# Last column chunk in pieces of 256, 128 and 128, and bulk loads split to choose the lane of the last store

## The chip, the cores and the metric

One core of a Trainium2 chip runs the whole program. The metric is the device time of one execution in microseconds (us); lower is better. The time is 1.9 us longer than the span of the trace (214.39 against 212.46 us for the profiled run of the kernel before). The kernel before took 214.23 us at first sight (median of 3 runs, 214.21 to 214.36). The experiments ran in three batches, each on one chip (a on chip 6; b1, b3, b4 and c on chip 1; b2 and d on chip 15), each with fresh runs of the kernel before.

## The reference

The input x has 2048 rows of 512 columns. Each row is layer-normalized to xn, and the output is x + A(xn) + B(xn):

```python
# A: a diagonal state-space model, 512 complex states, step over the 2048 rows
h = Lam_bar * h + Bu[t]                       # Bu = xn @ B_bar.T
y = 2.0 * (hseq @ Cmat.T).real + xn * Dskip
# B: a gated feed-forward layer with F = 1792
out = (silu(xn @ w1) * (xn @ w3)) @ w2
```

Inputs and output are bfloat16.

## The kernel before

The rows are worked on in four blocks of 512. For each block TensorE computes gate and up (`gu_ps`), the state input (`bu_ps`), and then the output (`y_ps`): per chunk of 128 rows, 14 matmuls of the feed-forward layer and 8 of the state are summed in one PSUM tile. VectorE adds the residual to the tile and a DMA stores it. The last chunk of the last block has nothing behind it that could hide its add and its store, so the kernel before already splits it into two column halves:

```python
        def finish(cl, dsl=slice(0, D), eng=nc.sync):
            o = outp.tile([P, D], BF16, name="o")
            nc.vector.tensor_tensor(out=o[:, dsl], in0=tiles[cl][:, dsl], in1=xn_blk[b][:, cl, dsl], op=ALU.add)
            eng.dma_start(out=ov[:, b * CPB + cl, dsl], in_=o[:, dsl])

        if b == NBLK - 1:
            # ... (chunks 0 to 2, whole)
            for i in range(2):
                dsl = slice(i * D // 2, (i + 1) * D // 2)
                from_gate(CPB - 1, dsl)      # 14 matmuls, own weights for each
                from_state(CPB - 1, dsl)     # 8 matmuls
                finish(CPB - 1, dsl, nc.sync if i == 0 else nc.scalar)
            return
```

The loads that matter here are issued on the SyncE queue; the DMA transposes of block 1 (`xnT<-xn`, four of them) follow them on the same queue:

```python
    def bulk_loads():
        # ... (w1, w3, x block 1, transposed B and C)
        nc.sync.dma_start(out=w2_sb, in_=B_w2.rearrange("(t p) d -> p t d", p=P))
        nc.sync.dma_start(out=dskip_row, in_=A_Dskip.partition_broadcast(P))

    def late_loads():        # issued after the transposes of block 1
        load_x(2)
        load_x(3)
```

Each DMA that SyncE or ScalarE issues signals its landing on one of eight semaphores. In the built instructions they are taken in turn, so the n-th DMA has lane n modulo 8. At the end of the program SyncE waits for all eight in a fixed order: lane 1, 2 (with 0), 3, 4, 5, 6, 7. The order is given by the framework; which lane the last store has depends only on how many DMAs were issued before it.

Of the kernel before, what the change touches and what calls it, by code (L numbers as in the profile page):

```python
# [16 lines left out]
P = 128  # L17
# [34 lines left out]
def kernel(  # L52
# [17 lines left out]
    nc = tc.nc  # L70
    _, S, D = A_x.shape
    F = B_w1.shape[1]
    PS = A_Lambda_re.shape[0]
    CPB = 4
# [5 lines left out]
    NFT = F // P  # L80
    LN_EPS = 1e-5
    FIRST = 3
    MID = 8
    NWARM = 9
    assert S == NBLK * TBLK and D == NDT * P and F == NFT * P and PS == NPT * P

    xv = A_x[0].rearrange("(c p) d -> p c d", p=P)
# [19 lines left out]
    w2_sb = const.tile([P, NFT, D], BF16, name="w2_sb")  # L107
# [17 lines left out]
    x_blk = [xpool.tile([P, CPB, D], BF16, name="x_blk") for _ in range(NBLK)]  # L125
# [3 lines left out]
    def load_w(f0, f1, eng1=nc.sync, eng3=nc.sync):  # L129
        eng1.dma_start(out=w1_sb[:, :, f0:f1], in_=w1v[:, :, f0:f1])  # L130
        eng3.dma_start(out=w3_sb[:, :, f0:f1], in_=w3v[:, :, f0:f1])

    def load_x(b):
        nc.sync.dma_start(out=x_blk[b], in_=xv[:, b * CPB:(b + 1) * CPB, :])

    for c in range(CPB):
        eng = nc.sync if c % 2 == 0 else nc.scalar
# [6 lines left out]
    def bulk_loads():  # L144
        nc.vector.tensor_copy(out=w1_sb[:, 0, FIRST * P:FIRST * P + 1], in_=mv_all[:, 1, 0:1])  # L145
        load_w(FIRST * P, MID * P)
        load_x(1)
        nc.sync.dma_start_transpose(out=bt_re, in_=A_B_re)
        nc.sync.dma_start_transpose(out=bt_im, in_=A_B_im)
        load_w(MID * P, 11 * P)  # L150
        load_w(11 * P, F)
        nc.sync.dma_start_transpose(out=ct_re, in_=A_C_re)
        nc.sync.dma_start_transpose(out=ct_im, in_=A_C_im)
        nc.sync.dma_start(out=w2_sb, in_=B_w2.rearrange("(t p) d -> p t d", p=P))
        nc.sync.dma_start(out=dskip_row, in_=A_Dskip.partition_broadcast(P))

    def late_loads():
        load_x(2)
        load_x(3)


    warm = const.tile([P, TBLK], BF16, name="warm")
# [3 lines left out]
    def keep_busy(n, cols):  # L166
        for _ in range(n):
            nc.tensor.matmul(out=wps[:, 0:cols], lhsT=warm[:, 0:P], rhs=warm[:, 0:cols], start=True, stop=True)

    keep_busy(NWARM, TBLK)  # L170
    nc.scalar.preload_act_table_set("natural_log_exp_and_others")
# [263 lines left out]
    def glu(b):  # L435
# [25 lines left out]
        if b == 0:  # L461
# [11 lines left out]
            ln_stats(0, 1)  # L473
            ln_first_rstd(1)
            bulk_loads()
            ln_apply(0, 0)
            ln_first_transpose(0)()
# [61 lines left out]
    def y(b):  # L539
        tiles = {}  # L540

        def from_gate(cl, dsl=slice(0, D)):
            if cl not in tiles or dsl.start:
                tiles[cl] = ps_y.tile([P, D], FP32, name="y_ps")
            for f in range(NFT):
                nc.tensor.matmul(out=tiles[cl][:, dsl], lhsT=hg_blk[b][:, f, cl * P:(cl + 1) * P],  # L546
                                 rhs=w2_sb[:, f, dsl], start=(f == 0), stop=False)

        def from_state(cl, dsl=slice(0, D)):
            for ri, ct in ((0, ct_re), (1, ct_im)):  # L550
                for pt in range(NPT):
                    nc.tensor.matmul(out=tiles[cl][:, dsl], lhsT=h_blk[b][:, pt, ri, cl * P:(cl + 1) * P],  # L552
                                     rhs=ct[:, pt, dsl], start=False, stop=(ri == 1 and pt == NPT - 1))
# [7 lines that stand above are left out]
            bg.flush(("ssm", b))  # L561
            bg.flush(("res", b))
            for cl in range(CPB - 1):
                from_gate(cl)
                from_state(cl)
                finish(cl)
            for i in range(2):
                dsl = slice(i * D // 2, (i + 1) * D // 2)
                from_gate(CPB - 1, dsl)
                from_state(CPB - 1, dsl)  # L570
                finish(CPB - 1, dsl, nc.sync if i == 0 else nc.scalar)
            return

        for cl in range(0, CPB, 2):
            from_gate(cl)
            bg.fill(2.8)
            from_gate(cl + 1)
            bg.fill(2.4)
            if cl == 0:
                bg.flush(("ssm", b))  # L580
                bg.flush(("res", b))
            from_state(cl)
            finish(cl)
            bg.fill(1.0)
            from_state(cl + 1)
            finish(cl + 1)
            bg.fill(1.0)
# [12 lines left out]
    bg.flush(("ln", 1))  # L600
    gate()
    late_loads()
    finish_c = [weight_c(pt) for pt in range(NPT)]
    res_tasks(0)
# [6 lines left out]
    bu(1)  # L611
    ln_scalar_engine(2)
    y(0)
    ssm_tasks(2)
    res_tasks(2)
    bu(2)
    gate = glu(2)
    gate()
    ln_scalar_engine(3)
    y(1)  # L620
    ssm_tasks(3)
    res_tasks(3)
    bu(3)
    gate = glu(3)
    gate()
    y(2)
    y(3)

# [29 lines left out]
```

## Time and profile before

| | value | where it stands |
|---|---|---|
| span | 212.46 us | page |
| TensorE busy | 207.2 us, 98% | page, part 1 |
| share of TensorE in the chain that ended last | 94% | page, part 4 |
| granted clock | 1.0 | page and runs |
| last matmul starts, end of span | 208.93, 212.46 us | records of the trace |

These lines of the page of the kernel before give the span, each engine's busy time and count, the chain that ended last by engine, and the stores (bytes of one, us from issue to landing); the last line, for the last store alone, is from the full list of DMA issues:

```profile
span 212.5 us, 2774 instructions
PE 207.2 (98%) x1056; PEld 99.0 (47%) x1056; DVE 155.7 (73%) x186; ACT 116.3 (55%) x219; POOL 24.7 (12%) x50
...
PE 94%; ACT 1%; DMA 1%; DVE 1%; issue 0%
...
out_dram<-o SPq DMA_DIRECT2D x15, 128.0 KB, 1.7
...
out_dram<-o ACTq DMA_DIRECT2D x1, 64.0 KB, 1.6
```

TensorE works almost all the time. A change can therefore gain only by shortening its stream, or what stands before its first or after its last matmul.

The timeline of the end of the kernel before (start, duration, engine, line, operation, output and input, count, and in brackets the idle time before it and what ended it):

```profile
206.63 1.69 PE L546 MATMUL y_ps<-w_sb,hgT 128*128 128x256 bf16 x14
206.83 0.42 DVE L557 TENSOR_TENSOR o<-y_ps,xn 128x256 bf16<-128x256 f32 x1 [1.71 <-PE y_ps L552]
207.29 0.33 SPq L558 DMA_DIRECT2D out_dram<-o  x1
...
208.60 0.60 PE L552 MATMUL y_ps<-ct_im,h 128*128 128x256 bf16 x4
209.24 0.42 DVE L557 TENSOR_TENSOR o<-y_ps,xn 128x256 bf16<-128x256 f32 x1 [1.98 <-PE y_ps L552]
209.69 0.37 ACTq L558 DMA_DIRECT2D out_dram<-o  x1
```

After the last matmul come an add of 0.42 us, the issue of a store, and then nothing that is counted as work, up to 212.46. What happens there can be read from the semaphore records of the same trace. "Lane" is the semaphore's place in the rotation; each line is the moment at which SyncE passed a wait:

```
209.693  last store issued (ACT queue), signals lane 3
211.269  the 16th and last of its landing signals arrives
211.286  SyncE passes lane 3
211.355  SyncE passes lane 4     (signalled long ago)
211.422  SyncE passes lane 5     (signalled long ago)
211.486  SyncE passes lane 6     (signalled long ago)
211.548  SyncE passes lane 7     (signalled long ago)
211.613  SyncE passes one more wait
211.688  SyncE gives its signal to the closing barrier
212.455  end of the span
```

The store takes 1.58 us from issue to landing. And the wait that it satisfies is followed by four others that were satisfied long before, and still take 0.062 to 0.069 us each, as SyncE reads them one after another.

### The profile page before, as it was taken

To read this page: it belongs to the slowest core of one execution; us is meant where nothing else is said; L and a number is where in the kernel's file an instruction comes from. 1 tells how busy PE (TensorE), PEld (TensorE's weight loads), DVE (VectorE), ACT (ScalarE), POOL (GpSimd) and SP (SyncE) were. 2 spreads that over 40 slices of the span, in tenths; PEclk is the share of its full clock that TensorE was granted. 3 is DMA by queue.
4 is the path that set the end of the run, shared out by engine and by line. 5 is a ranking of instruction groups with operands and counts; after the bars stand their busy time and mean duration, and the time that the engine had idled before them with its cause. 6 is when DMAs were issued, how large, how long until landed. Compare 5 with 4: busy or idle time off the path is not lost.

```text
span 212.5 us, 2774 instructions
## 1 busy us (share of the span) xinstructions
PE 207.2 (98%) x1056; PEld 99.0 (47%) x1056; DVE 155.7 (73%) x186; ACT 116.3 (55%) x219; POOL 24.7 (12%) x50
## 2 busy tenths in 40 slices
PE   7899999999999999999999999999999999999993
PEld 2874444444444444444444444444444444444462
DVE  3599799999938969899999897828999981121111
ACT  3699897799866764066666786036667620000000
POOL 7170289300000020000000012000000000000000
PEclk9999999999999999999999999999999999999999
DMA  6999999900000003400000001510000000100100
GB/s 167 323 227 213 287 286 213 244 2 0 3 0 0 0 0 77 98 25 0 0 0 5 0 0 25 123 52 0 2 0 0 3 0 3 46 25 29 48 25 26
DMA packets 26797, 13.68 MB, mean 64 GB/s; under 512 B 16544, under 2 KB 26784, under 8 KB 26784
## 3 DMA queue, kind: packets, MB, share of 16 engines
q1 hardware_dynamic: 25200, 12.78, 25.6%
q10 hardware_dynamic: 1488, 0.72, 1.2%
q8 instruction: 8, 0.13, 0.2%
q14 instruction: 5, 0.04, 0.1%
q0 software_dynamic: 96, 0.00, 0.0%
HBM read 7.74 MB, written 2.10 MB: 46 GB/s over the span
## 4 chain that ended last, share of the span: by engine, by line
PE 94%; ACT 1%; DMA 1%; DVE 1%; issue 0%
PE gu_ps L442 45%; PE y_ps L546 23%; PE y_ps L552 13%; PE bu_ps L370 12%; DMA x_blk<-in_A_x_dram 1%; PE bu_ps L442 1%; PE y_ps L209 1%; DVE stats L189 1%; ACT xnT L210 1%; ACT u L372 1%; ACT tabe L337 0%; DVE o L557 0%; DVE mv_all L190 0%; DVE xn L194 0%; DVE w_sb L145 0%
## 5 line engine op out<-in xcount | busy, mean ns | idle before, releaser
L442 PE MATMUL gu_ps<-xnT,w_sb 128*128 128x512 bf16 (+1 forms) x488 | 96.7, 358 | 0.2 <-ACT xnT L210 0.2
L442 PEld LDWEIGHTS <-w_sb 128*128 128x128 bf16 x520 | 46.9, 98 | 50.3 <-issue 0.4
L546 PE MATMUL y_ps<-w_sb,hgT 128*128 128x512 bf16 (+1 forms) x238 | 50.2, 366 | 0.0
L557 DVE TENSOR_TENSOR o<-y_ps,xn 128x512 bf16<-128x512 f32 (+1 forms) x17 | 11.2, 657 | 36.0 <-PE y_ps L552 36.0
L546 PEld LDWEIGHTS <-hgT 128*128 128x128 bf16 x238 | 23.3, 98 | 25.3
L372 ACT ACTIVATE u<-bu_ps 128x512 bf16<-128x512 f32 x32 | 19.1, 597 | 24.2 <-PE bu_ps L370 24.2
L406 DVE TENSOR_TENSOR_SCAN u<-rho,h,u 128x512 bf16<-128x512 f32 x24 | 29.5, 1270 | 0.2
L552 PEld LDWEIGHTS <-h 128*128 128x128 bf16 x136 | 13.3, 98 | 14.3
L552 PE MATMUL y_ps<-ct_re,h 128*128 128x512 bf16 (+1 forms) x68 | 16.6, 366 | 0.0
L552 PE MATMUL y_ps<-ct_im,h 128*128 128x512 bf16 (+1 forms) x68 | 16.6, 366 | 0.0
L370 PE MATMUL bu_ps<-xnT,bt_re 128*128 128x512 bf16 x64 | 16.4, 379 | 0.1
L370 PE MATMUL bu_ps<-xnT,bt_im 128*128 128x512 bf16 x64 | 16.4, 379 | 0.0
L393 DVE TENSOR_TENSOR p<-u,tabe 128x2048 bf16<-128x2048 bf16 x8 | 9.8, 1221 | 3.5 <-ACT u L372 3.4
L242 POOL TENSOR_SCALAR acc<-acc 128x4 f32<-128x4 f32 x2 | 1.0, 502 | 80.1 <-ACT xn L241 80.1
L411 DVE TENSOR_TENSOR p<-u,tabe 128x2048 bf16<-128x2048 bf16 x8 | 9.8, 1224 | 0.2
L418 DVE TENSOR_TENSOR h<-h,p 128x2048 bf16<-128x2048 bf16 x8 | 9.8, 1223 | 0.2
L396 DVE TENSOR_TENSOR u<-u,tabe 128x2048 bf16<-128x2048 bf16 x8 | 9.8, 1222 | 0.2
L400 DVE TENSOR_TENSOR u<-u,p 128x2048 bf16<-128x2048 bf16 x8 | 9.8, 1225 | 0.1
L370 PEld LDWEIGHTS <-bt_re 128*128 128x128 bf16 x64 | 6.3, 98 | 7.8 <-issue 0.3
L370 PEld LDWEIGHTS <-bt_im 128*128 128x128 bf16 x64 | 6.3, 98 | 7.5
L414 DVE TENSOR_TENSOR h<-u,tabe 128x2048 bf16<-128x2048 bf16 x8 | 9.8, 1219 | 0.0
L406 DVE TENSOR_TENSOR_SCAN u<-rho,u 128x512 bf16<-128x512 f32 x8 | 9.3, 1210 | 0.1
(172 smaller groups left out, 197.9 us busy)
## 6 DMA issues: line engine op xcount, KB each, us to landing
out_dram<-o SPq DMA_DIRECT2D x15, 128.0 KB, 1.7
w_sb<-in_B_w_dram SPq DMA_DIRECT2D x1, 1792.0 KB, 9.9
x_blk<-in_A_x_dram SPq DMA_DIRECT2D x3, 512.0 KB, 5.5
w_sb<-in_B_w_dram SPq DMA_DIRECT2D x4, 384.0 KB, 4.9
w_sb<-in_B_w_dram SPq DMA_DIRECT2D x2, 640.0 KB, 6.3
x_blk<-in_A_x_dram ACTq DMA_DIRECT2D x2, 128.0 KB, 3.1
x_blk<-in_A_x_dram SPq DMA_DIRECT2D x2, 128.0 KB, 2.7
w_sb<-in_B_w_dram SPq DMA_DIRECT2D x1, 256.0 KB, 5.8
```

The costliest lines, as they stand in the source:

```text
L370: nc.tensor.matmul(out=ps, lhsT=bt[:, dt, pt * P:(pt + 1) * P], rhs=xnT_blk[b][:, dt, :], start=(dt == 0), stop=(dt == NDT - 1))
L372: nc.scalar.activation(out=u[:, j, ri, :], in_=ps, func=ACT.Copy)
L393: nc.vector.tensor_tensor(out=st["p"], in0=st["g"], in1=tabe[:, psl, 1:3, :], op=ALU.mult)
L396: nc.vector.tensor_tensor(out=st["g"], in0=st["g"], in1=tabe[:, psl, 0:1, :].to_broadcast(FULL), op=ALU.mult)
L400: nc.vector.tensor_tensor(out=st["g"], in0=st["g"], in1=st["p"][:, :, ::-1, :], op=ALU.subtract)
L406: nc.vector.tensor_tensor_scan(out=v, data0=rho[:, pt:pt + 1].to_broadcast([P, TBLK]), data1=v, initial=init, op0=ALU.mult, op1=ALU.add)
L411: nc.vector.tensor_tensor(out=st["p"], in0=st["g"], in1=tabe[:, psl, 1:3, :], op=ALU.mult)
L414: nc.vector.tensor_tensor(out=h_blk[b][:, psl, :, :], in0=st["g"], in1=tabe[:, psl, 0:1, :].to_broadcast(FULL), op=ALU.mult)
L442: nc.tensor.matmul(out=ps[:, tsl], lhsT=w[:, dt, f * P:(f + 1) * P], rhs=xnT[:, dt, tsl], start=(dt == 0), stop=(dt == NDT - 1))
L546: nc.tensor.matmul(out=tiles[cl][:, dsl], lhsT=hg_blk[b][:, f, cl * P:(cl + 1) * P], rhs=w2_sb[:, f, dsl], start=(f == 0), stop=False)
L552: nc.tensor.matmul(out=tiles[cl][:, dsl], lhsT=h_blk[b][:, pt, ri, cl * P:(cl + 1) * P], rhs=ct[:, pt, dsl], start=False, stop=(ri == 1 an ...
L557: nc.vector.tensor_tensor(out=o[:, dsl], in0=tiles[cl][:, dsl], in1=xn_blk[b][:, cl, dsl], op=ALU.add)
```

## The change

The intent: a narrower last piece has a shorter add and a smaller store at the end, where nothing hides them. And with four more DMAs at or before the last store (w2 in two, x blocks 2 and 3 in two each, one more store), the last store moves four lanes on, from lane 3 to lane 7, the lane that is asked last. The other lanes can then be read while the store is still in flight.

```diff
+    LAST_COLS = ((0, D // 2), (D // 2, 3 * D // 4), (3 * D // 4, D))
...
-    def load_x(b):
-        nc.sync.dma_start(out=x_blk[b], in_=xv[:, b * CPB:(b + 1) * CPB, :])
+    def load_x(b, parts=1):
+        n = CPB // parts
+        for i in range(0, CPB, n):
+            nc.sync.dma_start(out=x_blk[b][:, i:i + n, :], in_=xv[:, b * CPB + i:b * CPB + i + n, :])
...
-        nc.sync.dma_start(out=w2_sb, in_=B_w2.rearrange("(t p) d -> p t d", p=P))
+        w2v = B_w2.rearrange("(t p) d -> p t d", p=P)
+        for sl in (slice(0, NFT // 2), slice(NFT // 2, NFT)):
+            nc.sync.dma_start(out=w2_sb[:, sl, :], in_=w2v[:, sl, :])
...
-        load_x(2)
-        load_x(3)
+        load_x(2, 2)
+        load_x(3, 2)
...
-            for i in range(2):
-                dsl = slice(i * D // 2, (i + 1) * D // 2)
+            for lo, hi in LAST_COLS:
+                dsl = slice(lo, hi)
                 from_gate(CPB - 1, dsl)
                 from_state(CPB - 1, dsl)
-                finish(CPB - 1, dsl, nc.sync if i == 0 else nc.scalar)
+                finish(CPB - 1, dsl, nc.scalar if hi == D else nc.sync)
```

## The prediction

> **What bounds the kernel now.** TensorE. The page has PE busy 207.2 of 212.5 us (98%); the chain that ended last is 94% PE; granted clock 1.0. So only what lengthens the PE stream, or stands after its last matmul, moves the time. The end, from the timeline with the trace's DMA landings and semaphore records (us from the span's start):
> - last 128x256 matmul starts 208.93; VectorE's last add starts 209.24, takes 0.42;
> - its store is issued on the ACT queue at 209.69; packets (128 of 512 B, 27 ns each) run 210.56 to 210.92; landed at 211.27, 1.58 us after issue;
> - SyncE's closing waits, about 0.067 us apart: 211.29, .36, .42, .49, .55, a drain at .61, the barrier signal at .69. DMA semaphores rotate over eight lanes, asked in lane order; the last store is on the first of these lanes, so four others, long satisfied, are read after it;
> - barrier and clean-up to 212.46.
> About 3.2 us after the last matmul that PE cannot hide.
>
> **What the change does.**
> 1. Lanes. w2 in two loads, x blocks 2 and 3 in two each, one more store: the last store moves four lanes on. In the built order it uses lane 7 instead of 3, the last one asked, so the other four are read while it is in flight: minus 4 x 0.067 = 0.27 us, all on the critical path.
> 2. Last add 128 wide instead of 256: 0.69 us at 512 columns, 0.42 at 256, so on that line about 0.29: minus 0.13.
> 3. Store rows of 256 B: packets of 256 B took 18 ns elsewhere in this trace against 27, eight per engine: minus 0.07 (estimate); the rest of the 1.58 us stays. The Trainium skill ("DMA: Bandwidth & Descriptors", Specifications) says that below 512 B the DMA does a read-modify-write; no store here is that small yet, so this could eat the 0.07 or more.
> 4. PE: 44 matmuls of 128 columns for 22 of 256. Spacing in this trace: 0.0558 us (opening quarters, weights loaded for each) against 0.1092: plus 0.05. The skill ("TensorE: Matmul & The Clock Gate", Back-to-back issue gap) gives about 81 ns at 128 with weight loads; the trace shows 56, which I use. At 81 the change would lose 1.1 us.
> 5. Loads: same bytes. The split of w2 puts one more issue (about 0.6 us on SyncE) ahead of block 1's four transposes. They land by 39.53 and TensorE begins that block at 39.77: only 0.2 us of slack. The queue is backed up by w2's data there, so I expect little (mean 0.05, at worst 0.5). The x loads have 30 us of slack.
>
> Sum: -0.27 - 0.13 - 0.07 + 0.05 + 0.05 = about -0.4: **213.85 us**, range 213.6 to 214.25. Faster by over 2%: 0.5%; within 2%: 99%; slower by over 2%: 0.5%.
>
> **What would show it.** (1) Landing of the last store to SyncE's barrier signal 0.15 us instead of 0.42, to the end of the span 0.92 instead of 1.19. (2) Last add near 0.29. (3) Issue to landing near 1.5. (4) 128-column matmuls 0.056 apart, no gap between pieces; the third piece waits neither for its output buffer (the first piece's store lands near 208.8, needed 209.3) nor for PSUM. (5) No PE gap near 39.8.
>
> **What would make it wrong.** 128-column matmuls spaced by weight loads; a slow 256 B store; a stall of block 1 behind the split w2; a chip that differs by 0.1 us.

## The result

213.94 us (median of 6 runs, 213.66 to 214.15), against 214.27 us before (6 runs, 214.21 to 214.39). The ratio is 0.9984, 95% interval 0.9971 to 0.9997. Ratios in this document are the mean time of one kernel's fast runs over that of the other's fast runs of the same rounds, so not quite the ratio of the medians quoted. By the line of 2% that the prediction uses, the two kernels count as the same.

The predicted 213.85 us missed by 0.09 us. The effect is small and single runs scatter as much, so that close an agreement is partly luck, and the traces have to say whether the reasons were right.

The lines of the changed kernel's page (and list of DMA issues) that answer to those shown of before:

```profile
span 212.0 us, 2826 instructions
PE 206.5 (97%) x1078; PEld 98.8 (47%) x1078; DVE 155.9 (74%) x187; ACT 116.3 (55%) x219; POOL 24.6 (12%) x50
...
PE 94%; DVE 2%; DMA 1%; ACT 1%; issue 0%
...
out_dram<-o SPq DMA_DIRECT2D x15, 128.0 KB, 1.7
...
out_dram<-o ACTq DMA_DIRECT2D x1, 32.0 KB, 1.5
```

TensorE has 22 matmuls more (1078 against 1056) and is still the chain. The timeline of the end of the changed kernel, in the same columns as before:

```profile
206.63 0.94 PE L551 MATMUL y_ps<-w_sb,hgT 128*128 128x128 bf16 x14
206.83 0.42 DVE L562 TENSOR_TENSOR o<-y_ps,xn 128x256 bf16<-128x256 f32 x1 [1.71 <-PE y_ps L557]
...
208.06 0.29 DVE L562 TENSOR_TENSOR o<-y_ps,xn 128x128 bf16<-128x128 f32 x1 [0.80 <-PE y_ps L557]
...
208.86 0.39 PE L557 MATMUL y_ps<-ct_im,h 128*128 128x128 bf16 x4
209.29 0.29 DVE L562 TENSOR_TENSOR o<-y_ps,xn 128x128 bf16<-128x128 f32 x1 [0.94 <-PE y_ps L557]
209.61 0.37 ACTq L563 DMA_DIRECT2D out_dram<-o  x1
```

The last add is 0.29 us instead of 0.42. The third piece's add waited for TensorE alone, as the bracket says; the landing signals of the first piece's store, whose buffer it reuses, were complete at 208.81. The semaphore records of the same trace, as above:

```
208.758 to 209.009  SyncE passes lanes 1 to 5, while the store is not yet issued
209.612  last store issued (ACT queue), signals lane 7
209.849  SyncE passes lane 6 (the second piece's store)
211.104  the last of the landing signals of lane 7 arrives
211.121  SyncE passes lane 7
211.186  SyncE passes one more wait
211.255  SyncE gives its signal to the closing barrier
212.028  end of the span
```

From the landing to the barrier signal it is now 0.151 us instead of 0.419. The four reads have moved out of the way, as intended.

The upper part of the two traces differs at one place. First the kernel before, the chain that ended last in order of time (start, duration, what):

```profile
27.68 1.89 PE bu_ps L370 x8
29.57 34.53 PE gu_ps L442 x160
64.10 6.91 PE bu_ps L370 x32
```

Then the changed kernel:

```profile
27.57 1.89 PE bu_ps L375 x8
29.45 34.65 PE gu_ps L447 x160
64.10 6.91 PE bu_ps L375 x32
```

The changed kernel came to 29.45 us 0.12 us earlier and lost it again before 64.10. The records of single matmuls show where. They run 0.216 us apart, but between 39.435 and 39.768 us lies one interval of 0.333 us, 0.117 too much. The matmul at 39.768 is the first of block 1. The last transpose of block 1 had landed at 39.677. In the kernel before it landed at 39.525 and was needed at 39.767, so there was no gap. The 0.12 us at the start belongs to the run, not to the kernel, as the 14 traces below show.

### The profile page after: what moved, and what is told of

Read it like the earlier page. It is cut to its first block, busy times and chain, and to the rows that moved or that the text cites. A ratio compares the mean times of both kernels' runs of the same rounds, so it can differ in the third digit from the quotient of the medians.

```text
span 212.0 us, 2826 instructions
## 1 busy us (share of the span) xinstructions
PE 206.5 (97%) x1078; PEld 98.8 (47%) x1078; DVE 155.9 (74%) x187; ACT 116.3 (55%) x219; POOL 24.6 (12%) x50
## 4 chain that ended last, share of the span: by engine, by line
PE 94%; DVE 2%; DMA 1%; ACT 1%; issue 0%
PE gu_ps L447 45%; PE y_ps L551 23%; PE y_ps L557 13%; PE bu_ps L375 12%; DMA x_blk<-in_A_x_dram 1%; DVE stats L194 1%; PE bu_ps L447 1%; ACT u L377 1%; PE y_ps L214 0%; DVE xn L199 0%; ACT tabe L342 0%; ACT xnT L215 0%; DVE mv_all L195 0%; DVE o L562 0%; DVE w_sb L148 0%
## 5 line engine op out<-in xcount | busy, mean ns | idle before, releaser
L551 PE MATMUL y_ps<-w_sb,hgT 128*128 128x512 bf16 (+2 forms) x252 | 50.4, 355 | 0.0
L457 ACT ACTIVATE u<-gu_ps 128x512 bf16<-128x512 f32 x55 | 33.3, 605 | 11.4 <-PE gu_ps L447 10.8
L456 ACT ACTIVATE g<-gu_ps 128x512 bf16<-128x512 f32 x55 | 33.1, 602 | 9.5 <-PE gu_ps L447 9.5
L562 DVE TENSOR_TENSOR o<-y_ps,xn 128x512 bf16<-128x512 f32 (+2 forms) x18 | 11.3, 629 | 35.8 <-PE y_ps L557 35.8
L463 DVE TENSOR_TENSOR hgT<-g,u 128x1024 bf16<-128x1024 bf16 x28 | 19.0, 682 | 5.8 <-ACT u L457 5.8
L557 PE MATMUL y_ps<-ct_im,h 128*128 128x512 bf16 (+2 forms) x72 | 16.8, 355 | 0.0
L557 PE MATMUL y_ps<-ct_re,h 128*128 128x512 bf16 (+2 forms) x72 | 16.8, 355 | 0.0
```

The source lines that it names most:

```text
L456: nc.scalar.activation(out=g16[:, f % 2, :], in_=g_ps, func=ACT.Silu)
L457: nc.scalar.activation(out=u16[:, f % 2, :], in_=u_ps, func=ACT.Copy)
L463: nc.vector.tensor_tensor(out=hgT[:, f - 1:f + 1, :], in0=g16, in1=u16, op=ALU.mult)
L551: nc.tensor.matmul(out=tiles[cl][:, dsl], lhsT=hg_blk[b][:, f, cl * P:(cl + 1) * P], rhs=w2_sb[:, f, dsl], start=(f == 0), stop=False)
L557: nc.tensor.matmul(out=tiles[cl][:, dsl], lhsT=h_blk[b][:, pt, ri, cl * P:(cl + 1) * P], rhs=ct[:, pt, dsl], start=False, stop=(ri == 1 an ...
```

## The experiments

All traces can be compared piece by piece once the start is taken out. The first matmul of the feed-forward part (`gu_ps`) began between 6.90 and 7.33 us in the 14 traces, though nothing of the change stands before it. It is 7.16 and 6.90 for the kernel before and for b2 below, which differs from it only later, and 7.04, 7.18 and 7.26 in three traces of the changed kernel. So the start scatters from run to run, by as much as the effect. From that matmul to the end of the span, the traces repeat within about 0.02 us, also on another chip: 205.293 and 205.284 for the kernel before and b2, 204.863 and 204.878 for the two traces of the changed kernel without a gap.

The traces also say what the start is made of. The first chunk of x landed between 3.24 and 3.52 us. From that landing to the first `gu_ps` matmul it took 3.64 to 3.65 us in the seven traces whose clock records show TensorE's full clock granted by 5.81 us, and longer the later that moment came: 3.67 with 6.00, 3.81 with 6.38, 3.93 with 7.20. (In the trace of before, warm-up matmuls of 512 columns started 0.427 us apart ahead of that moment; later ones of 512 columns start 0.216 us apart.) This is an agreement over 14 traces. No run was made to test it.

The table below has this stretch and its parts, all in us, read from the records of the traces:

| run | pieces; lane of last store | first `gu_ps` to last matmul's start | last matmul's start to add | last add | store, issue to landing | landing to SyncE's barrier signal | first `gu_ps` to end |
|---|---|---|---|---|---|---|---|
| before | 256, 256; 3 | 201.764 | 0.310 | 0.425 | 1.576 | 0.419 | 205.293 |
| changed | 256, 128, 128; 7 | 201.989 (gap 0.117) | 0.256 | 0.292 | 1.492 | 0.151 | 204.985 |
| a1_pieces_only | 256, 128, 128; 4 | 201.877 | 0.257 | 0.292 | 1.497 | 0.328 | 205.055 |
| a2_lanes_only | 256, 256; 7 | 201.769 | 0.309 | 0.425 | 1.571 | 0.145 | 205.019 |
| a3_w2_whole | 256, 128, 128; 7 | 201.877 | 0.256 | 0.291 | 1.491 | 0.140 | 204.855 |
| a4_lane_first | 256, 128, 128; 1 | 201.879 | 0.256 | 0.292 | 1.515 | 0.522 | 205.269 |
| c_after_again | as changed | 201.877 | 0.257 | 0.292 | 1.492 | 0.140 | 204.863 |
| b1_w2_late | 256, 128, 128; 7 | 201.879 | 0.257 | 0.292 | 1.489 | 0.145 | 204.860 |
| b3_best | 384, 128; 7 | 201.824 | 0.257 | 0.292 | 1.435 | 0.140 | 204.744 |
| b4_last64 | 256, 192, 64; 7 | 201.901 | 0.232 | 0.224 | 1.462 | 0.151 | 204.776 |
| d1_best64 | 256, 192, 64; 7 | 201.901 | 0.231 | 0.224 | 1.413 | 0.140 | 204.709 |
| d2_last32 | 256, 224, 32; 7 | 202.116 | 0.213 | 0.192 | 1.437 | 0.145 | 204.903 |
| b2_before_w2_late | 256, 256; 3 | 201.768 | 0.311 | 0.424 | 1.574 | 0.407 | 205.284 |
| d3_after_third | as changed | 201.879 | 0.257 | 0.292 | 1.496 | 0.151 | 204.878 |

What is left in each row is the time from the add's end to the issue of the store (0.03) and from the barrier signal to the end (0.77, the same in all).

The main theory was that of the prediction: the gain is the sum of the lane (0.27), the add (0.13) and the store (0.08), less 0.05 of TensorE. The first rival gives everything to the narrow piece and nothing to the order of the waits; a second gives it to the finer loads. For the gap near 39.8 us, theory S blamed the split of w2.

### a1_pieces_only: the column pieces without the split loads

```diff
-        for sl in (slice(0, NFT // 2), slice(NFT // 2, NFT)):
-            nc.sync.dma_start(out=w2_sb[:, sl, :], in_=w2v[:, sl, :])
+        nc.sync.dma_start(out=w2_sb, in_=B_w2.rearrange("(t p) d -> p t d", p=P))
...
-        load_x(2, 2)
-        load_x(3, 2)
+        load_x(2)
+        load_x(3)
```

> The column pieces 256, 128, 128 alone; all loads as before, so the last store moves one lane on (lane 4), and three lanes stay to be read after it. Main theory (closing waits cost 0.067 us for each lane read after the last store): last add 0.29 us (-0.13), store 1.49 us instead of 1.58 (-0.08), PE +0.05, one lane less -0.07: about -0.23 us against before, near 214.05; landing of the last store to SyncE's barrier signal 0.35 us. Rival (order of the waits is worth nothing, the narrow last piece is all of the gain): -0.33 us, the same time as the changed kernel. No PE gap near 39.8 us, as w2 is one load.

Measured: 214.18 us against 214.42 before in the same rounds, ratio 0.9990 (0.9978 to 1.0002); by the trace 0.24 us less than before from the first `gu_ps` matmul to the end. The add, the store and TensorE are those of the changed kernel, but landing to barrier signal is 0.328, as three lanes are still read afterwards. The pieces alone are not all of the gain; the rival falls. No gap near 39.8 us.

### a2_lanes_only: the lane without the pieces

```diff
-    LAST_COLS = ((0, D // 2), (D // 2, 3 * D // 4), (3 * D // 4, D))
+    LAST_COLS = ((0, D // 2), (D // 2, D))
...
-        load_x(2, 2)
-        load_x(3, 2)
+        load_x(2, 4)
+        load_x(3)
```

> Two pieces of 256 as before, but loads split (w2 in two, x block 2 in four) so that the last store is on lane 7, asked last. Main theory: landing to SyncE's barrier signal 0.15 us instead of 0.42, so -0.27 us in the tail, add 0.42 and store 1.58 unchanged; PE may lose 0.1 us near 39.8 as w2 is split: -0.17 to -0.27 against before. Rival (lane order worth nothing): 0.

Measured: 214.19 us against 214.42, ratio 0.9992 (0.9980 to 1.0004); by the trace 0.27 us less than before. The timeline of its end shows the same work as the kernel before:

```profile
208.54 0.60 PE L557 MATMUL y_ps<-ct_im,h 128*128 128x256 bf16 x4
209.18 0.42 DVE L562 TENSOR_TENSOR o<-y_ps,xn 128x256 bf16<-128x256 f32 x1 [1.98 <-PE y_ps L557]
209.64 0.36 ACTq L563 DMA_DIRECT2D out_dram<-o  x1
```

Add and store cost what they cost before (0.425 and 1.571), and the 0.27 us stands entirely between landing and barrier signal: 0.145 instead of 0.419. The two intervals of the whole times of a1 and a2 reach 1, so it is the traces that separate these effects and not the times. w2 is split here, and there is no gap near 39.8 us.

The parts add up: a1 gained 0.24, of which 0.09 is its own step of one lane (0.419 to 0.328), so the pieces are worth 0.15; with the 0.27 of a2 that is 0.42. The changed kernel without a gap (c_after_again) gained 205.293 - 204.863 = 0.43.

### a4_lane_first: the lane that is asked first

```diff
-        load_x(3, 2)
+        load_x(3, 4)
```

> As the changed kernel, but x block 3 in four loads instead of two: the last store is on lane 1, the one asked FIRST. Wrong on purpose. Main theory: six lanes are read after it instead of none, +0.40 us against the changed kernel, landing to SyncE's barrier signal about 0.55 us instead of 0.15; total near or above before. Rival (finer bulk loads are what helps): the same time as the changed kernel or faster.

Measured: 214.68 us against 214.42, ratio 1.0031 (1.0003 to 1.0059; one of its six runs took 216.58, which pulls the mean up). By the trace it is 205.269 from the first `gu_ps` matmul to the end, 0.02 us under before; what made that run longer stands ahead of that matmul (7.33 us, the latest of all traces, against 7.16) and outside the span (2.06 us against 1.93). Two more loads, of the same bytes, undo the gain. Its semaphore records:

```
211.306  the last landing signal of lane 1 arrives
211.322  SyncE passes lane 1
211.381, .447, .512, .573, .632, .694   lanes 2, 3, 4, 5, 6, 7
211.759  one more wait
211.828  barrier signal
```

This closes the series: with 0, 3, 4 and 6 lanes still to be read after the last store, landing to barrier signal is 0.14 to 0.15, 0.33, 0.41 to 0.42 and 0.52 us. From lane 7 to lane 1 it is (0.522 - 0.145) / 6 = 0.063 us for each. The finer loads as such help nothing, so the second rival falls too.

### a3_w2_whole: is it the split of w2 that makes the gap?

```diff
-        for sl in (slice(0, NFT // 2), slice(NFT // 2, NFT)):
-            nc.sync.dma_start(out=w2_sb[:, sl, :], in_=w2v[:, sl, :])
+        nc.sync.dma_start(out=w2_sb, in_=B_w2.rearrange("(t p) d -> p t d", p=P))
...
-        load_x(2, 2)
-        load_x(3, 2)
+        load_x(2, 4)
+        load_x(3)
```

> As the changed kernel (three pieces, last store on lane 7), but w2 in one load again and x block 2 in four instead, x block 3 whole. Theory S (the PE gap of 0.12 us at 39.44 to 39.77 comes from the split of w2 putting one more issue ahead of the transposes of block 1): the gap is gone, last transpose landed by 39.55, about 0.1 us faster than the changed kernel, 213.8. Rival (the gap comes because the start was 0.12 us earlier in that run and the transposes land when they land, whatever the split): a gap also here whenever the block starts before about 39.75, time within 0.05 of the changed kernel.

Measured: 213.88 us against 214.42, ratio 0.9977 (0.9965 to 0.9989). No gap; last transpose of block 1 landed at 38.16. Alone this looks like theory S, but the kernels of the same batch with w2 split have none either, with the landing at 39.12 (a2) and 39.20 (a4). So it decides nothing by itself, which is why the next two were made.

### c_after_again and d3_after_third: the changed kernel twice more

> The changed kernel again, unaltered, for the same chip and rounds as the next three, and for a second trace. Expected 0.3 to 0.45 us under before. If the PE gap near 39.8 us belongs to the changed kernel it is there again (0.1 us); if it was a chance of that run (the last transpose of block 1 landed at 38.2 to 39.7 in six traces, with w2 whole and split alike), it is mostly absent. Tail as before: landing to barrier signal 0.15 us, store 1.49, add 0.29.

Measured: 213.90 us against 214.41, ratio 0.9969 (0.9954 to 0.9984). No gap; last transpose landed at 37.62.

> The changed kernel once more, for the same chip and rounds as the three above: 0.3 to 0.5 us under before, first gu_ps matmul to end 204.86 if there is no gap near 39.8 us, more by the gap if there is one.

Measured: 214.02 us against 214.34, ratio 0.9981 (0.9965 to 0.9997). No gap; landed at 39.29. So one trace of three of the changed kernel has the gap. Theory S has fallen as it was put, with the split alone making the gap. Over the traces in which w2 is queued ahead of the transposes, the last landing is at 38.2, 39.1 and 39.5 us with w2 whole, and at 37.6, 37.7, 38.8, 39.1, 39.2, 39.3 and 39.7 with w2 split. The ranges overlap, and the gap comes when a late landing meets an early start. The split has a small cost of its own: from the first issue of w2 to the first issue of a transpose SyncE took 1.89 to 1.95 us with w2 whole (3 traces) and 1.92 to 2.40 with w2 split (7 traces, mean 2.13). These 0.2 us are small against the 2 us over which the landings scatter, but whether the one gap (2.09 us in its trace) would have come without them, no run shows.

### b1_w2_late: w2 behind the transposes

```diff
     def bulk_loads():
         # ...
-        for sl in (slice(0, NFT // 2), slice(NFT // 2, NFT)):
-            nc.sync.dma_start(out=w2_sb[:, sl, :], in_=w2v[:, sl, :])
-        nc.sync.dma_start(out=dskip_row, in_=A_Dskip.partition_broadcast(P))
     def late_loads():
+        # the same three loads, w2v defined as above
         load_x(2, 2)
```

> The changed kernel with the loads of w2 and dskip_row issued after the four transposes of block 1 instead of before them (same number of loads, last store still on lane 7). If w2's 1.8 MB queued ahead is what makes those transposes land at 38 to 39.7 us, they land before 35 here and no run can have the gap near 39.8: the time is that of the changed kernel without a gap, 0 to 0.1 us under it, with less spread. If something else delays them, they land as late as before.

Measured: 213.95 us against 214.41, ratio 0.9972 (0.9956 to 0.9987); the changed kernel had 0.9969 in the same rounds. The SyncE queue of the changed kernel (first trace), in order of time:

```profile
26.16 1.19 SPq L159 DMA_DIRECT2D w_sb<-in_B_w_dram  x2
27.40 0.75 SPq L160 DMA_DIRECT2D dskip_row<-in_A_Dskip_dram  x1
28.25 9.16 SPq L218 DMA_TRANSPOSE xnT<-xn  x4
```

The SyncE queue of b1:

```profile
26.55 7.02 SPq L218 DMA_TRANSPOSE xnT<-xn  x4
33.62 1.19 SPq L161 DMA_DIRECT2D w_sb<-in_B_w_dram  x2
34.85 0.56 SPq L162 DMA_DIRECT2D dskip_row<-in_A_Dskip_dram  x1
```

In b1 the last transpose landed at 34.78, some 5 us before it can be needed (39.77 in the traces above). So having w2 and dskip_row (they were moved together) queued ahead is indeed what makes the transposes late; whether w2 is whole or in two is not seen in the landings. But the time did not fall and its spread (213.58 to 214.15) did not shrink, which the expectation had hoped for. The gap is too rare and too small to be seen in six runs, against a start that scatters by 0.4 us.

### b2_before_w2_late: the same for the kernel before

```diff
     def bulk_loads():
         # ...
-        nc.sync.dma_start(out=w2_sb, in_=B_w2.rearrange("(t p) d -> p t d", p=P))
-        nc.sync.dma_start(out=dskip_row, in_=A_Dskip.partition_broadcast(P))
     def late_loads():
+        # the same two loads
         load_x(2)
```

> Control: the kernel before with only w2 and dskip_row moved behind the transposes of block 1. If that queue costs the kernel before nothing (no gap in its trace, last transpose 0.24 us ahead of need): same time as before, first gu_ps matmul to end 205.30 as in before. If it hides a stall in many runs: up to 0.1 us faster.

Measured: 214.33 us against 214.34, ratio 0.9998 (0.9984 to 1.0012); 205.284 from the first `gu_ps` matmul to the end, against 205.293. The last transpose landed at 32.94. Having w2 queued ahead cost the kernel before nothing that these runs show.

### b4_last64: a last piece of 64 columns

```diff
-    LAST_COLS = ((0, D // 2), (D // 2, 3 * D // 4), (3 * D // 4, D))
+    LAST_COLS = ((0, D // 2), (D // 2, 7 * D // 8), (7 * D // 8, D))
```

> The changed kernel with pieces 256, 192, 64. Does narrowing go on paying? Theory W (below 128 columns the weight load of each matmul sets the spacing, about 0.055 us): 22 matmuls of 64 columns cost as much as 22 of 128, PE +0.58 us against the changed kernel, add about -0.07, store about -0.04: +0.45 us, slower. Rival (spacing keeps to the columns, about 0.03 us): -0.1 us.

Measured: 213.69 us against 214.41, ratio 0.9964 (0.9948 to 0.9980). My theory W fell. Groups of instructions in the end of this run, by form (busy time and mean ns of one):

```profile
L551 PE MATMUL y_ps<-w_sb,hgT 128*128 128x192 bf16 x14 | 1.3, 246 | 0.0
L551 PE MATMUL y_ps<-w_sb,hgT 128*128 128x64 bf16 x14 | 0.6, 193 | 0.0
...
L562 DVE TENSOR_TENSOR o<-y_ps,xn 128x64 bf16<-128x64 f32 x1 | 0.2, 224 | 0.3 <-PE y_ps L557 0.3
```

The 14 matmuls of 64 columns were busy for 0.6 us together: they started 0.029 us apart, each with its own load of 128x128 weights. The last add took 0.224 us and the store of 128-byte rows 1.462. From the first `gu_ps` matmul to the end this is 0.09 us under the changed kernel.

### d2_last32: a last piece of 32 columns

```diff
+    LAST_COLS = ((0, D // 2), (D // 2, 15 * D // 16), (15 * D // 16, D))   # in place of the changed kernel's
```

> The changed kernel with pieces 256, 224, 32. Where does narrowing stop? 64 columns ran 0.029 us apart, so no weight-load limit of 0.055 was met. If a floor near 0.029 holds below 64 columns: PE +0.29 us against the 256/192/64 kernel, add about -0.03, store about -0.02, first gu_ps matmul to end about 205.0, worse than the changed kernel's 204.86. If the spacing keeps following the columns (about 0.016): about 204.71, better than 204.77.

Measured: 213.91 us against 214.34, ratio 0.9980 (0.9964 to 0.9995). Here narrowing stops: the 32-column matmuls started 0.025 us apart, hardly less than the 0.029 of 64 columns. TensorE reached its last matmul 0.215 us later than in b4. Add and store gave back 0.03 each. 204.903 in all: worse than 204.776, and no better than the changed kernel without a gap.

The same group in this run, from the timeline (start, duration):

```profile
208.60 0.51 PE L551 MATMUL y_ps<-w_sb,hgT 128*128 128x32 bf16 x14
```

It took 0.51 us, with half the columns of b4's group (0.57 us in the timeline there).

### b3_best and d1_best64: all that helps together

b3 has two pieces (22 matmuls fewer than the changed kernel), w2 and dskip_row late, and the last store on the SyncE queue; d1 is the same with the pieces 256, 192, 64.

```diff
# b3_best
-    LAST_COLS = ((0, D // 2), (D // 2, 3 * D // 4), (3 * D // 4, D))
+    LAST_COLS = ((0, 3 * D // 4), (3 * D // 4, D))
...
     def late_loads():
+        # w2 (one load) and dskip_row here
-        load_x(2, 2)
+        load_x(2, 4)
         load_x(3, 2)
...
-                finish(CPB - 1, dsl, nc.scalar if hi == D else nc.sync)
+                finish(CPB - 1, dsl, nc.sync)
# d1_best64, against b3_best
-    LAST_COLS = ((0, 3 * D // 4), (3 * D // 4, D))
+    LAST_COLS = ((0, D // 2), (D // 2, 7 * D // 8), (7 * D // 8, D))
-        load_x(3, 2)
+        load_x(3)
```

> Meant to beat both: last chunk in two pieces of 384 and 128 columns, w2 (whole) and dskip_row behind the transposes, x block 2 in four loads so that the last store is on lane 7, and the last store issued on the SyncE queue. Against the changed kernel: PE -0.05 (22 matmuls less for the same columns), store -0.04 (the 256-byte store on the SyncE queue took 1.45 us, that on the ACT queue 1.49), no gap near 39.8. Tail otherwise the same. So 0.1 to 0.2 us under the changed kernel; near 0.5 under before.

Measured: 213.78 us against 214.41, ratio 0.9966 (0.9952 to 0.9981); 204.744 by the trace, 0.12 under the changed kernel (c_after_again): TensorE -0.05, store -0.06, as expected.

> What the runs so far point to, together: pieces 256, 192, 64, w2 (whole) and dskip_row behind the transposes, x block 2 in four loads so that the last store is on lane 7, last store on the SyncE queue. From the first matmul of the feed-forward part (gu_ps) to the end of the span: before 205.30 us, changed 204.86 (without its gap), 256/192/64 alone 204.77, and the SyncE queue's store 0.05 less (1.44 against 1.49): 204.72. So about 0.14 us under the changed kernel and 0.58 under before, in a run whose start is the same. Rival: the third piece's store waits on the SyncE queue behind the second's, and nothing is gained over 256/192/64 on the ACT queue (204.77).

Measured: 213.85 us against 214.34, ratio 0.9976 (0.9961 to 0.9990); the changed kernel had 214.02 in the same rounds. By the trace 204.709, the shortest of all and within 0.01 of the sum that was expected. The store on the SyncE queue took 1.413 us, against 1.462 on the ACT queue for the same 128-byte rows.

So d1 beats the kernel before by 0.58 us from the first `gu_ps` matmul to the end, and the changed kernel by 0.15. Of the whole times, only the first is certain: b3, b4 and d1 are 0.6, 0.7 and 0.5 us under before, while their lead over the changed kernel of the same rounds (0.1 to 0.2 us) is inside the spread that the start makes.

## Why the prediction was right, and the one step of it that was not borne out

The time was within the range, and 0.09 us above the point. Term by term:

| term | predicted | measured, changed against before |
|---|---|---|
| four lanes read earlier | -0.27 | 0.151 - 0.419 = -0.27 |
| last add | -0.13 | 0.292 - 0.425 = -0.13 |
| store | -0.07 | 1.492 - 1.576 = -0.08 |
| TensorE | +0.05 | +0.113 to the last matmul's start (gap taken out: c_after_again), -0.053 from there to the add: +0.06 |
| stall of block 1 | +0.05 on average | +0.117 in one trace of three, 0 in two |
| sum | -0.37 | -0.43 without the gap, -0.31 with it |

- **Lanes.** Right in mechanism and size. The series of a1, a2 and a4 shows it as a cost for each lane still to be read, whatever the pieces are.
- **Add and store.** Right. The warning that rows below 512 B could be slow did not come true for this store: the Trainium skill ("DMA: Bandwidth & Descriptors", Specifications) names 512 B as the smallest transfer for full rate, but on the ACT queue the last store of 128 rows landed after 1.57 to 1.58 us with rows of 512 B (3 traces), 1.49 to 1.52 with 256 B (7 traces), and 1.462 and 1.437 with 128 and 64 B (one trace each, a step no larger than the scatter of the 256 B stores). The bytes of the store shrank with its rows, so this is no test of the rate. The store's packets took 27, 18, 12.5 and 10.5 ns for these four sizes: less time each, but fewer bytes per ns (19, 15, 10 and 6). They ran for only 0.2 to 0.35 us of the 1.4 to 1.6.
- **TensorE.** Right: matmuls of 128 columns ran 0.056 us apart with their own weights, as in the opening part of the trace of before. Trusting the trace over the 81 ns of the skill ("TensorE: Matmul & The Clock Gate", Back-to-back issue gap) was what kept the sign of the prediction right.
- **Stall of block 1.** Of the right size on average (0.117 us in one trace of three), which with one event is luck; of the signs that the prediction listed, (5), no gap near 39.8 us, failed in the first trace. Of its two reasons, the extra issue of about 0.6 us ahead of the transposes measured 0.2 us on average, and a2, a4, b4, d2 and two further traces of the changed kernel have the split and no gap, with landings that overlap those with w2 whole. The other, that the queue is backed up by w2's data, fits: with w2 and dskip_row behind the transposes, in b1, b2, b3 and d1, they land at 32.9 to 34.8 us instead of 37.6 to 39.7. The kernel before has the same exposure, with 0.24 us to spare in its trace. What share the split had in the one gap stays open.
- **What was missed.** The prediction allowed for "a chip that differs by 0.1 us". In fact the start of a single run moves by up to 0.43 us (6.90 to 7.33), whichever kernel it is. That is why three comparisons of the same two kernels gave 0.33, 0.51 and 0.32 us between the medians, while the traces give 0.43 (0.31 with the gap). The part of the time outside the span scatters too, by 0.2 us (1.9 to 2.1). The traces put the start's scatter down to the landing of the first x chunk and to the moment of the full clock (see above); no run changed either.

## What to carry to other kernels

When one engine is busy 98% of the time, look at what stands after its last instruction, and at the closing waits too: a wait that was satisfied long ago still costs its read (about 0.063 us here) if it is asked after the last one that matters, so let the last store signal the semaphore that is asked last. Narrow the last piece of work until the busy engine's own floor for small instructions eats the gain, here between 64 and 32 columns. In d2 the 32-column matmuls started 0.025 us apart against 0.029 for 64 columns, while the wider piece before them grew. And when an effect is as small as the scatter of the start, compare traces from a fixed instruction onwards, not whole times.

## What the Trainium skill lacked or had wrong

- "TensorE: Matmul & The Clock Gate", Back-to-back issue gap: it gives about 81 ns (128 columns) and 131 ns (512) between matmuls in a stream with weight loads. Every such stream here ran at about 56 and 216 ns, the values that this section calls isolated (elsewhere the page has them for back-to-back matmuls, so it disagrees with itself). Its row for 1 to 64 columns (about 60 cycles, 25 ns) fits 32 columns (25 ns here), but 64 columns took 29 ns, which is what the section's formula for the isolated gap gives.
- "DMA: Bandwidth & Descriptors", Specifications: it says that below 512 B the DMA does a read-modify-write, but not what that means for a lone store. Here such a store did not get slower in all, with its bytes shrinking too: 1.576, 1.492, 1.462, 1.437 us for rows of 512, 256, 128, 64 B. No run here shows whether a read-modify-write took place.
- The same page, Issuing engine by pattern, puts SyncE and ScalarE together as generally the faster way to issue a DMA, with no difference between the two. The last store landed 0.05 us sooner from the SyncE queue than from the ACT queue (1.413 against 1.462 us for rows of 128 B, 1.435 against 1.492 for 256 B). Stores of 512 B rows agree: 1.52 to 1.54 us from SyncE in 13 traces, 1.57 to 1.58 from ACT in 3.
- No page that I read says what the order of the closing waits costs: about 0.063 us for each satisfied wait that is read after the last store. "Advanced Engine Details and Errata", Network/Comms, has 50 to 100 ns for the read of a semaphore by a sequencer; the 63 ns here lie within that.
